# A two-stage Strassen kernel: third weight form from SyncE, products moved, token sums reordered

## Chip, cores and metric

The kernel runs on one core of a Trainium2 chip. The metric is the device time of one execution in microseconds; here the medians of several runs, and beside them one profiled execution with its own time.

## What is computed

An attention block without softmax (a retention with a decay per head) is followed by a feed-forward block with a product of two branches:

```python
# q, k, v: (8, 8, 576, 64) float32
scores = q @ k.T / sqrt(64)
ret = scores * where(i >= j, gamma[h] ** (i - j), 0)
x = (ret @ v)                      # brought to (8 * 576, 8 * 64) = (4608, 512)
a = x @ w1                         # w1, w2: (512, 1024)
b = x @ w2
out = ((a * b) @ w3) @ w_out       # w3: (1024, 1024), w_out: (1024, 512)
```

All of it is float32. The kernel forms w3 @ w_out once (tile w3o), so that a token passes two products: the "up" products x @ w1 and x @ w2, whose elementwise product is kept in tile ab, and the "down" product ab @ w3o.

## The kernel before

**Tiling.** The 8 batches are taken two at a time; a pair has 5 chunks of tokens (one of 64, four of 128), numbered g = 0 to 19 over the four pairs. For a chunk the attention part loads q, k and v, scales them, transposes q and k, and makes scores (`score`, L224, with the mask product L236 on DVE), the running state (`state`, L240) and the output x (`pv`, L278), which lands in tiles xT of 192 tokens of both batches. Twelve such blocks of tokens exist. The first four go through a plain Strassen product (`up`, L507); the other eight in four *groups* of two blocks, gr = 0 to 3, through two nested levels of Strassen (`up2`, L1008). All edits are in the part that handles groups, from about 350 us on.

**A group.** `token_forms` (L942) makes the sums of the two blocks of x that Strassen needs, all on POOL (`tt`, L948). First the differences inside xT, then six sums into tile T (which is a part of ra), then one difference b12 in place and two sums into tile E, then the sum E4 (the function `rest`, L964; for group 0 it is called later by hand, L1182, for the others inside), then a difference inside T, and six sums from T into tiles U. E and E4 serve the steps P1, P2, P7 and P3 of a half (below), T and U the steps P6, P4 and P5.

A group then has 14 *steps* (n = 0 to 13; two halves h of seven Strassen products in the order P1, P2, P6, P7, P4, P5, P3). A step (`up2`) has seven inner products on PE (L1028), each with two weight blocks, accumulated in PSUM tiles p1, p5 (pool acc, 5 banks) and p6 (pool seed, 2 banks). DVE adds the banks to tile c (one of four cc tiles in rotation, `plus`, L1035), ACT copies, and POOL adds earlier cc tiles into this one (`more`, L1031). The last inner product of a step and its adds (the inner function `rest`, L1082) are put behind and issued inside the next step by `finish` (L991). In the step P5, called the *joined* step here (`both` is not empty), the result goes into two cc tiles at once, so POOL has four sums instead of two and DVE two adds per bank (L1038).

**Products of results.** When a step completes a quarter of a and b, entries are added to the list `results` (L1090); `multiply(most)` (L995) takes up to that many of them and issues for each the DVE product L1003, ab <- cc * cc, whose two inputs are in SBUF. `up2` calls it near its end (L1076): at most 1 in a joined step, at most 2 in the others. A cc tile is free again after its second product.

**Weights.** The 14 weight forms (896 KB each) were stored in HBM (`kept`). A ring of three slots in SBUF holds the forms of this step and the next ones. `open_second` (L921) makes the ring and issues the first two forms on SP; after that every step issues one form on POOL (`next_forms`, L935, called at L1053). POOL's queue also holds the scaling of q (`scale_blocks`, L175, instruction L181) and loads of v and k (L93). SP's queue holds, right behind the first forms, the loads of q for the next chunks, 16 pieces per chunk (`load_blocks`, L160, L171). The program gives SP's transfers eight completion semaphores in turn.

**Output stage.** After the 14 steps come three `down` calls (L625). Each has seven products on PE (L637) over two tiles of 128 tokens, in the order 1 (A11), 7 (S3), 2 (A12), 6 (S2), 5 (S1), 4 (A22), 3 (S4). The sums S3, S2, S1 and S4 of ab are DVE instructions L607, L611, L613 and L679, with both inputs in SBUF. S2 and S1 need products of results from the last two steps.

**The order.** The order on each engine is written out by hand (`manual_schedule`): the loop from L1196 deals a number of steps to each chunk g (`dealt`, L1195: 3, 4, 4, 3, 3, 7, 7, 3, 7, 7), so a group's steps end at g = 13, 16 and 19, and the last group's after the loop. At the first three of these (`if g in ready`, L1225) the loop issues `pv`, then `finish` and `multiply` for everything that is left, then the state and the scores of the next chunk (there is none at g = 19), then it queues the next group. In the next round `token_forms` for the next group follows behind the first `down`. In the first `down` behind the last steps (L668 to L675) `finish` and `multiply` are called again, which matters for the last group alone. Queues run in order, and each engine stops at the first instruction whose input isn't there.

Of the kernel before, what the change touches and what calls it, by code (L numbers as in the profile page):

```python
# [19 lines left out]
def kernel(  # L20
# [875 lines left out]
    def weight_of(slot, nm, w):  # L896
        lo = {"A11": 0, "A12": P, "S3": 4 * P, "A22": 5 * P, "S1": 8 * P, "S4": 9 * P, "S2": 12 * P}[nm]
        lo += w * (P if nm == "S2" else 2 * P)
        return slot[:, lo:lo + P]

    order = ("P1", "P2", "P6", "P7", "P4", "P5", "P3")
    ring, sent, steps, free = [], [0], [0], []
    groups = [(m, m + 1) for m in range(4, len(every), 2)]

    def flush():
        while spread:
            spread.pop(0)()
# [13 lines left out]
    def open_second():  # L921
        nonlocal acc
        flush()
        acc_part.close()
        acc = ctx.enter_context(tc.tile_pool(name="acc", bufs=5, space=PSUM, reuse_waits="tile"))
        pools["seed"] = ctx.enter_context(tc.tile_pool(name="seed", bufs=2, space=PSUM, reuse_waits="tile"))
        ra = wp.tile([P, 32 * P], F32, tag="wA1", name="ra")
        cs = wp.tile([P, 2, 4, 2, TB], F32, tag="wS1", name="cc")
        ring.extend([ra[:, :FORM], ra[:, FORM:2 * FORM]])
        free.extend(cs[:, j] for j in range(2))  # L930
        live["first"] = [ra[:, 2 * FORM + j * DM // 2:2 * FORM + (j + 1) * DM // 2] for j in range(2)]
        for _ in range(2):
            next_forms(nc.sync)

    def next_forms(engine=nc.gpsimd):  # L935
        n = sent[0]
        if n < 14 * len(groups):
            nm = NAMES.index(OPERANDS[order[n % 7]][0])
            engine.dma_start(ring[n % 3], kept[n % 14 // 7][nm])  # L939
            sent[0] += 1  # L940

    def token_forms(gr):  # L942

        x = [live["xT", m] for m in groups[gr]]
        T, E, U = live["T2"], live["E"], live["U"]

        def tt(out, in0, in1, op=ALU.subtract):
            nc.gpsimd.tensor_tensor(out=out, in0=in0, in1=in1, op=op)  # L948

        for s in range(2):  # L950
            tt(x[s][:, :2, 1], x[s][:, 2:, 1], x[s][:, :2, 1])
        b11, b21 = (x[0].rearrange("p (r c) b t -> p r c b t", c=2)[:, :, c] for c in range(2))
        b12, b22 = (x[1].rearrange("p (r c) b t -> p r c b t", c=2)[:, :, c] for c in range(2))
        sums = [(T[:, s, 1], x[s][:, :2, 1], x[s][:, :2, 0], ALU.add) for s in range(2)]
        sums += [(T[:, s, 0], x[s][:, 2:, 1], T[:, s, 1]) for s in range(2)]
        sums += [(T[:, s, 2], x[s][:, 2:, 0], T[:, s, 1]) for s in range(2)]
        for args in sums:
            tt(*args)
        tt(b12, b22, b12)
        tt(E[:, 1], b12, b11, ALU.add)  # L960
        tt(E[:, 0], b22, E[:, 1])
        forms = {}

        def rest(b11=b11, b21=b21, b22=b22, b12=b12):  # L964
            if "E4" not in live:
                live["E4"] = pools["carry"].tile([P, KF, P], F32, tag="carry", name="e4").rearrange(
                    "p f n -> p (f n)")[:, :4 * TB].rearrange("p (r b t) -> p r b t", r=2, b=2)
            E4 = live["E4"]
            tt(E4, b21, E[:, 1])
            for nm, (r, b) in {"B11": (0, 0), "B21": (1, 0), "T3": (0, 1), "B22": (1, 1)}.items():  # L970
                forms[nm] = {"B11": b11[:, r, b], "B21": b21[:, r, b], "B22": b22[:, r, b], "T3": b12[:, r, b],
                             "T1": E[:, 0, r, b], "T2": E[:, 1, r, b], "-T4": E4[:, r, b]}

        if gr:
            rest()
        tt(T[:, 1, :, 0], T[:, 1, :, 1], T[:, 1, :, 0])
        for k in (slice(0, 2), 2):
            u = [U[j] if k != 2 else (U[3][:, 0], U[3][:, 1], U[4][:, 0])[j] for j in range(3)]
            b11, b21, b12, b22 = (T[:, s, k, c] for s in range(2) for c in range(2))
            tt(u[1], b12, b11, ALU.add)  # L980
            tt(u[0], b22, u[1])
            tt(u[2], b21, u[1])
            for i, nm in enumerate(("T1", "T2") if k != 2 else ("-T4",)):
                part = [y[:, i] if k != 2 else y for y in (b11, b21, b22, b12, *u)]
                forms[nm] = dict(zip(("B11", "B21", "B22", "T3", "T1", "T2", "-T4"), part))
        live["B2", gr] = forms
        return rest
# [20 lines left out]
    def up2(gr, n):  # L1008

        h, key = n // 7, order[n % 7]  # L1010
        slot = ring[steps[0] % 3]
        if not steps[0]:

            for _ in range(2):
                t = pools["seed"].tile([P, 2, TB], F32, tag="seed", name="seed")
                nc.tensor.matmul(t.rearrange("p a t -> p (a t)"), ident, live["w3o"][:, 0, :2 * TB],
                                 start=True, stop=True)
        B = live["B2", gr][OPERANDS[key][1]]
        steps[0] += 1
        c = free.pop(0)  # L1020
        sums2[key] = c
        add = {"P2": "P1", "P6": "P1", "P7": "P6", "P4": "P7", "P3": "P6"}.get(key)
        add = sums2[add] if add else None
        both = [sums2["P6"], sums2["P7"]] if key == "P5" else []

        def product(ps, a, b, new=False):
            for w in range(2):
                nc.tensor.matmul(ps[:, w, :], weight_of(slot, a, w), B[b], start=(new and w == 0), stop=True,  # L1028
                                 skip_group_check=True)

        def more(into, of, part):  # L1031
            o, i = into[:, part], of[:, part]
            nc.gpsimd.tensor_tensor(out=o, in0=o, in1=i, op=ALU.add)  # L1033

        def plus(ps, j, with_add=None):  # L1035
            if both:
                for o in both:
                    nc.vector.tensor_add(o[:, j], ps, o[:, j])  # L1038
            elif with_add is not None:
                nc.vector.tensor_add(c[:, j], ps, with_add[:, j])  # L1040
            else:
                nc.scalar.copy(c[:, j], ps)

        p1 = acc.tile([P, 2, TB], F32, tag="acc", name="up")
        product(p1, "A11", "B11", True)
        p6 = pools["seed"].tile([P, 2, TB], F32, tag="seed", name="seed")
        nc.scalar.copy(p6, p1)  # L1047
        store()
        p5 = acc.tile([P, 2, TB], F32, tag="acc", name="up")
        product(p5, "S1", "T1", True)  # L1050
        nc.scalar.copy(c[:, 3], p5)  # L1051
        finish()
        next_forms()  # L1053
        if loads:
            loads.pop(0)()
        product(p6, "S2", "T2")
        nc.scalar.copy(c[:, 1], p6)
        if beside:
            beside.pop(0)()
        for o in both:  # L1060
            more(o, c, 3)
        if add is not None:
            more(c, add, 3)
        product(p1, "A12", "B21")
        plus(p1, 0, add)
        product(p5, "S4", "B22")
        if add is not None:
            more(c, add, 1)
        for o in both:
            more(o, c, 1)  # L1070
        product(p6, "S3", "T3")
        plus(p6, 3, c)
        plus(p5, 1, c)
        if both:
            free.append(c)
        multiply(1 if both else 2)  # L1076
        if n == 13:
            results.append((gr, h, 0, 1, c, 1))
        if aside:
            aside.pop(0)()  # L1080

        def rest():  # L1082
            product(p6, "A22", "-T4")
            plus(p6, 2, add)
            if key in ("P6", "P3"):
                free.append(sums2["P1" if key == "P6" else "P6"])
            done = {"P2": (0, 0), "P4": (1, 0), "P5": (1, 1), "P3": (0, 1)}.get(key)
            if done:
                z = sums2["P7"] if key == "P5" else c
                results.extend((gr, h, *done, z, half) for half in ((0,) if n == 13 else (1, 0)))  # L1090

        behind.append(rest)

    real = (up, up2, down)

    def add_group(gr):
        X, Y = groups[gr]
        todo.extend((up2, gr, n) for n in range(14))
        todo.extend([(down, (X, 0), (X, 1)), (down, (X, 2), (Y, 2)), (down, (Y, 0), (Y, 1))])
# [96 lines left out]
    for g in range(2 * NC, G):  # L1196
# [27 lines left out]
        pv(g)()  # L1224
        if g in ready:  # L1225
            finish()
            multiply()
        if g + 2 < G:
            load(g + 2, "v", nc.gpsimd)
            if (g + 2) % NC != NC - 1:  # L1230
# [1 line left out]
        if g + 1 < G:  # L1232
            state(g + 1)
            score(g + 1)
        if g in ready:
            add_group(ready[g])
        if g == G - 1:
            token_forms(ready[g])
# [45 lines left out]
```

## Time and profile before

| | |
|---|---|
| median of 3 runs | 850.87 us (846.77 to 853.91) |
| the profiled execution's own time | 850.68 us |
| its span, first to last instruction | 848.9 us |
| mean granted TensorE clock | 0.989 |
| idle time of PE, by the span and its busy time | 29.6 us |
| idle time of PE before the product L1028 behind POOL sums into e | 3.7 us |
| products of results L1003 on DVE | 64, mean 796 ns |
| sums for token forms of 384 elements, xT and ra into ra (16) | mean 1237 ns |
| forms of weights issued by SP and by POOL | 2 and 54 |
| a form from issue to landing, median | 5.0 us |

The profile follows one execution instruction by instruction. A row of a timeline or a group names the source line, the engine, the operation, the tile written and the tiles read, the shape, and then the count, the duration and the idle time of the engine just before it with what ended that idle time. PE's list of waits adds these idle times up by pairs of lines. A wait for several semaphores is put down to the one that came last. The table of windows gives, for stretches of time, the busy time of an engine, the share of the full TensorE clock that was granted, and what the DMA engines moved.

### The profile page before, as it was taken

To read this page: it belongs to the slowest core of one execution; us is meant where nothing else is said; L and a number is where in the kernel's file an instruction comes from. 1 tells how busy PE (TensorE), PEld (TensorE's weight loads), DVE (VectorE), ACT (ScalarE), POOL (GpSimd) and SP (SyncE) were. 2 spreads that over 40 slices of the span, in tenths; PEclk is the share of its full clock that TensorE was granted. 3 is DMA by queue.
4 is the path that set the end of the run, shared out by engine and by line. 5 is a ranking of instruction groups with operands and counts; after the bars stand their busy time and mean duration, and the time that the engine had idled before them with its cause. 6 is when DMAs were issued, how large, how long until landed. Compare 5 with 4: busy or idle time off the path is not lost.

```text
span 848.9 us, 15774 instructions
## 1 busy us (share of the span) xinstructions
PE 819.3 (97%) x6085; PEld 738.1 (87%) x6085; DVE 541.2 (64%) x887; ACT 283.2 (33%) x581; POOL 325.6 (38%) x330
## 2 busy tenths in 40 slices
PE   7899999999999999979998999999999999999998
PEld 6889999644989998869998889998899998899987
DVE  4899999991644477615657644759735768446653
ACT  4777556670111101033343024342034331033300
POOL 1100010001104181395545935556916468445500
PEclk8999999999999999999999999999999999999999
DMA  9995454436046487979786147787275452245401
GB/s 193 217 224 128 77 150 125 126 98 112 1 98 125 75 220 251 307 209 220 190 229 167 44 93 228 201 238 177 58 156 183 140 208 69 77 148 189 159 25 51
DMA packets 201291, 126.96 MB, mean 150 GB/s; under 512 B 161272, under 2 KB 183032, under 8 KB 201216
## 3 DMA queue, kind: packets, MB, share of 16 engines
q1 hardware_dynamic: 170944, 50.14, 29.1%
q0 software_dynamic: 11776, 63.71, 23.0%
q10 hardware_dynamic: 18496, 12.10, 5.3%
q8 instruction: 48, 0.79, 0.4%
q14 instruction: 27, 0.22, 0.1%
HBM read 103.62 MB, written 22.28 MB: 148 GB/s over the span
## 4 chain that ended last, share of the span: by engine, by line
PE 79%; DMA 7%; DVE 7%; issue 3%; SPq 2%; ACT 1%; POOL 0%; ACTq 0%; DVEq 0%; POOLq 0%
PE po L637 24%; PE up L1028 15%; PE up L524 13%; PE seed L1028 11%; PE ps L477 6%; DMA ld_v<-in_v_dram 3%; PE xps L299 3%; PE sc L233 3%; DMA ra<-kept 2%; PE xps L274 1%; SPq L171 1%; DVE c L529 1%; DVE ab L1003 1%; DMA bl_q<-in_q_dram 1%; PE st L255 1%
## 5 line engine op out<-in xcount | busy, mean ns | idle before, releaser
L637 PE MATMUL po<-w3o,ab 128*128 128x256 f32 x552 | 125.0, 381 | 1.4 <-DVE ot L641 0.5
L637 PEld LDWEIGHTS po<-w3o,ab 128*128 128x128 f32 x552 | 103.9, 190 | 17.4 <-DVE ot L641 1.2
L1033 POOL TENSOR_TENSOR cc<-cc 128x384 f32<-128x384 f32 x112 | 109.3, 1001 | 4.1 <-ACT cc L1051 2.4
L1040 DVE TENSOR_TENSOR cc<-seed,cc 128x384 f32<-128x384 f32 x88 | 48.7, 553 | 72.9 <-PE seed L1028 68.5
L181 POOL TENSOR_TENSOR bl_q<-bl_q,gqs 128x512 f32<-128x512 f32 (+1 forms) x30 | 30.8, 1048 | 127.7 <-DMA bl_q<-in_q_dram 91.8
L939 POOL DMA_DIRECT2D ra<-kept x54 | 30.6, 567 | 124.1 <-PE seed L1028 103.3
L1028 PE MATMUL up<-xT,ra 128*128 128x192 f32 x384 | 74.2, 330 | 0.6 <-DMA ra<-kept 0.6
L1040 DVE TENSOR_TENSOR cc<-up,cc 128x384 f32<-128x384 f32 x88 | 48.4, 550 | 36.8 <-PE up L1028 31.5
L524 PE MATMUL up<-xT,wA 128*128 128x192 f32 x384 | 70.4, 327 | 0.0
L529 DVE TENSOR_TENSOR c<-up,c 128x384 f32<-128x384 f32 x80 | 44.0, 550 | 38.9 <-PE up L524 38.3
L1028 PEld LDWEIGHTS up<-xT,ra 128*128 128x128 f32 x384 | 64.4, 192 | 2.0 <-DMA ra<-kept 0.9
L236 DVE TENSOR_TENSOR pm<-sc,mask 128x512 f32<-128x512 f32 (+1 forms) x80 | 45.4, 626 | 32.1 <-PE sc L233 32.0
L637 PE MATMUL po<-wB,forms 128*128 128x256 f32 x288 | 65.2, 379 | 0.5 <-DVE forms L611 0.5
L524 PEld LDWEIGHTS up<-xT,wA 128*128 128x128 f32 x384 | 63.4, 190 | 1.1 <-issue 0.5
L637 PEld LDWEIGHTS po<-wB,forms 128*128 128x128 f32 x288 | 54.6, 190 | 8.2 <-PE po L637 0.8
L1047 ACT COPY seed<-up 128x384 f32<-128x384 f32 x56 | 25.9, 463 | 100.1 <-PE up L1028 46.6
L1028 PE MATMUL seed<-e,ra 128*128 128x192 f32 x256 | 52.9, 337 | 5.2 <-DVE cc L1040 2.9
L1028 PE MATMUL up<-ra 128*128 128x192 f32 x288 | 55.1, 328 | 1.9 <-DMA ra<-kept 1.9
L477 PE MATMUL ps<-wo,w3T 128*128 128x512 f32 x128 | 55.1, 592 | 0.0
L204 POOL TENSOR_TENSOR ld_v<-ld_v,gk 128x1024 f32<-128x1024 f32 (+1 forms) x9 | 17.1, 1899 | 90.5 <-DMA ld_v<-in_v_dram 90.5
L679 DVE TENSOR_TENSOR ab<-ab,forms 128x512 f32<-128x512 f32 x17 | 17.1, 1008 | 53.3 <-PE po L637 53.3
L1028 PEld LDWEIGHTS seed<-e,ra 128*128 128x128 f32 x256 | 43.7, 194 | 7.8 <-DVE cc L1040 3.6
(127 smaller groups left out, 1597.2 us busy)
## 6 DMA issues: line engine op xcount, KB each, us to landing
ra<-kept POOLq DMA_DIRECT2D x54, 896.0 KB, 5.0
raw<-in_moe_w_dram SPq DMA_DIRECT2D x72, 128.0 KB, 3.0
bl_q<-in_q_dram SPq DMA_DIRECT2D x216, 32.0 KB, 3.2
out_dram<-ot ACTq DMA_DIRECT2D x54, 128.0 KB, 2.3
bl_k<-in_k_dram SPq DMA_DIRECT2D x136, 32.0 KB, 2.4
raw<-in_moe_w_dram SPq DMA_DIRECT2D x16, 256.0 KB, 6.0
ld_k<-in_k_dram SPq DMA_DIRECT2D x8, 512.0 KB, 5.9
raw<-in_moe_w_out_dram SPq DMA_DIRECT2D x32, 128.0 KB, 2.7
```

What stands on the lines that cost most here:

```text
L181: nc.gpsimd.tensor_tensor(out=part, in0=part, in1=gqs[:, :, n0:n0 + n].unsqueeze(3).to_broadcast([P, NP, n, BL]), op=ALU.mult)
L233: nc.tensor.matmul(sc[j][:sz, p, :sz], kT[hs, b, p, :sz], qT[hs, b, p, :sz], start=True, stop=True)
L236: nc.vector.tensor_mul(pm[:sz, b, j, :, :sz], sc[j][:sz, :, :sz], mask[:sz, :sz].unsqueeze(1).to_broadcast([sz, NP, sz]))
L477: nc.tensor.matmul(ps, live["w3T", ft][:, g, :], live["wo"][:, g, :], start=(g == 0), stop=(g == KF - 1))
L524: nc.tensor.matmul(ps[:, w, :], a[:, w, r, :], b[:, r, :], start=(new and w == r == 0), stop=(w == r == 1), skip_group_check=True)
L529: nc.vector.tensor_add(c[:, to], ps, c[:, sb])
L637: nc.tensor.matmul(ps[nm], a[A][:, f, :], live["W"][B][:, f, :], start=(f == 0 and not on), stop=(f == NP - 1), skip_group_check=True)
L939: engine.dma_start(ring[n % 3], kept[n % 14 // 7][nm])
L1028: nc.tensor.matmul(ps[:, w, :], weight_of(slot, a, w), B[b], start=(new and w == 0), stop=True, skip_group_check=True)
L1033: nc.gpsimd.tensor_tensor(out=o, in0=o, in1=i, op=ALU.add)
L1040: nc.vector.tensor_add(c[:, j], ps, with_add[:, j])
L1047: nc.scalar.copy(p6, p1)
```

## The change

It has four parts. `open_second` issues three forms on SP instead of two, and `up2` issues a form only if fewer than two are ahead, so that the first step issues none and all later ones are as they were. In `token_forms` the six sums into T come behind b12, E and (but for group 0) E4, instead of ahead of them; since they then read the changed b12, the difference inside T (one POOL instruction of 576 elements) falls away. A joined step issues no product of results; the entry is taken by one of the next steps, so four instead of three are left at the end of a group. And at the end of a group the products that are left come behind the state and scores of the next chunk, so on DVE behind the four mask products L236.

```diff
@@ open_second
-        for _ in range(2):
+        for _ in range(3):
             next_forms(nc.sync)
@@ token_forms
         sums += [(T[:, s, 2], x[s][:, 2:, 0], T[:, s, 1]) for s in range(2)]
-        for args in sums:
-            tt(*args)
+
         tt(b12, b22, b12)
         tt(E[:, 1], b12, b11, ALU.add)
         tt(E[:, 0], b22, E[:, 1])
...
         if gr:
             rest()
-        tt(T[:, 1, :, 0], T[:, 1, :, 1], T[:, 1, :, 0])
+        for args in sums:
+            tt(*args)
         for k in (slice(0, 2), 2):
@@ up2
         finish()
-        next_forms()
+        if sent[0] < steps[0] + 2:
+            next_forms()
         if loads:
...
             free.append(c)
-        multiply(1 if both else 2)
+        if not both:
+            multiply(2)
         if n == 13:
@@ the loop over chunks
         if g in ready:
             finish()
-            multiply()
         if g + 2 < G:
             load(g + 2, "v", nc.gpsimd)
...
             state(g + 1)
             score(g + 1)
         if g in ready:
+            multiply()
             add_group(ready[g])
```

## The prediction

> **What bounds the kernel now.** I read part 1 of the page first, then the list of waits of PE, then the timelines of PE, POOL and DVE around each wait, and the table of windows for the granted clock.
>
> ```profile
> PE 819.3 (97%) x6085; PEld 738.1 (87%) x6085; DVE 541.2 (64%) x887; ACT 283.2 (33%) x581; POOL 325.6 (38%) x330
> ```
>
> PE is the bound. The change removes no matmul, so it acts on PE's idle time and on the clock alone. From 360 us on, where all edits lie, the waits that the edits can reach are these (line, what ended the wait, total us, times, longest):
>
> ```profile
> PE seed L1028 <- DVE cc L1040: 2.9, 3, 1.3
> PE up L1028 <- DMA ra<-kept: 2.5, 2, 1.9
> PE up L1028 <- POOL e L948: 2.2, 1, 2.2
> ...
> PE sc L233 <- DVE kT L190: 1.7, 1, 1.7
> PE seed L1028 <- POOL e L948: 1.5, 1, 1.5
> ...
> PE sc L233 <- DVE cc L1040: 0.7, 1, 0.7
> ...
> PE po L637 <- DVE forms L611: 0.5, 1, 0.5
> ```
>
> PE's timeline places them. At the start of group 0 PE waits 2.25 us until 369.74 (POOL e), 1.50 until 377.73 (POOL e, the last token form) and 1.91 until 383.16 (weight form 2). The DVE waits follow the joined step P5: in group 0's end 0.78 (462.73) and 1.72 (465.37), in group 1's middle 0.68 (546.22), in its end 0.79 (585.10), in group 3's middle 1.28 (776.93).
>
> Behind them stands a product of results (L1003) that usually takes 0.55 us and sometimes 2.7:
>
> ```profile
> L1003 DVE TENSOR_TENSOR ab<-cc x64: 529/549/2743, 390.7 to 811.9; 128x384 f32<-128x384 f32 x64
> ```
>
> Five of the eight in joined steps took 2.7 (456.96, 540.90, 579.32, 662.23, 772.28), while POOL added cc tiles. How DVE and POOL hinder each other is best seen at the end of group 2 (DVE, then POOL; the columns are start, duration, instruction):
>
> ```profile
> 706.34 3.58 DVE L1003 TENSOR_TENSOR ab<-cc 128x384 f32<-128x384 f32 x3
> 709.96 1.37 DVE L611 TENSOR_TENSOR forms<-ab 128x512 f32<-128x512 f32 x1
> ...
> 715.80 1.96 DVE L611 TENSOR_TENSOR forms<-ab 128x512 f32<-128x512 f32 x1
> ```
>
> ```profile
> 709.47 5.53 POOL L948 TENSOR_TENSOR ra<-xT,ra 128x384 f32<-128x384 f32 x4
> 715.08 2.13 POOL L948 TENSOR_TENSOR xT<-xT 128x768 f32<-128x768 f32 x1
> ```
>
> L611 takes 0.69 us beside an idle POOL, 1.37 beside POOL's 384-element sums, 1.96 beside a 768-element one: the two engines take turns, one whole instruction each. The masks (L236, one input from PSUM) take 0.68 beside the same POOL work: they do not take turns.
>
> [...] Here 2.25 us of idling sufficed. In the table of windows (PE busy, granted clock, DMA share, GB/s) the clock falls behind the first wait:
>
> ```profile
> 366.00:368.00 2.00, 1.49 (x7) 1.00 0.95 389
> 368.00:370.00 2.00, 0.26 (x1) 1.00 1.10 224
> 370.00:372.00 2.00, 2.00 (x8) 0.50 0.35 58
> ```
>
> It falls so too in 384 to 386 and 466 to 468; the 1.28 us at 776.9 cost no clock. [...] the windows 366 to 368 and 380 to 382 show 389 and 386 GB/s while forms move, for either issuer.
>
> **Part by part.** The sum is made against the profiled execution (span 848.9, its own time 850.68; the median of the three runs is 850.87, so nothing is to be shifted).
>
> *Start of group 0 (third form, token order).* POOL's sums of xT into ra take 1.95+3.86 = 5.8 us; put behind E they let E end at 369.68-5.8 = 363.9, before PE comes at 367.5. That wait goes, but PE then stands at -T4's form (E4), which ends only 1.4 us earlier (377.68 to 376.3, the 576-element sum of 1.40 that is gone). So the first two waits give 1.4, and PE sits 4.4 us in one piece. Form 2 leaves SP at about 363.6 instead of POOL at 377.62; at 896 KB and 389 GB/s it is in by 372, and PE wants it at about 379.7: the 1.91 go. Together 3.3. What is late next: SP's 16 pieces of bl_q for chunk 11, 363.55 to 374.62, now queue behind 0.9 MB more, 2.4 us; they land near 380, and POOL's in-order queue holds behind them: scaling 2.08 (to 382.1), a form's issue 0.6, the first cc sum 0.98 (383.7), then DVE's add 0.56 (384.2), which frees the seed bank for PE's last product of the second step. Before it began at 385.44, and half clock cost it another 0.8. Gain 385.4+0.8-384.2 = **2.0**; between 0.3 (pieces 2 us later still) and 4 (not late, clock kept). SP's extra issue is 0.34, POOL's saved one 0.6. The test in L1053 drops one issue in the first step only. The shorter token sums of groups 1 to 3 (1.4 to 1.9 us of POOL each) are worth nothing: the forms are ready at 495.2 and wanted at 510.3, and similarly later; without that cover they would give that much.
>
> *Joined steps.* One product fewer in each of 8. In the middles (n=5) two PE waits go: 0.68+1.28 = **2.0**. The others had no wait behind them. The product reappears in steps 6 to 8, in DVE gaps of 0.77: nothing.
>
> *Ends of groups (n=12, 13, then the output stage).* Now four products are left instead of three, and they come after the masks. Group 2 is the clearest: it has no score, so the products start at 706.4 as before; but POOL, after its xT difference (to 706.97), now has 768-element sums: 1.80 each plus 0.32 for DVE's turn. Products end at 707.3, 709.4, 711.5, 713.7; L611 at 713.7+1.80+0.44 = 716.0. PE's product of S2 needs L611: 711.48 before, 716.0 after, **+4.5**. L613 (717.4) is then hidden by that product. A 5 us wait halves the clock for about 3.4 us, +1.7; half of it counted: **+5.4**.
> Group 1: PE arrives 0.79 sooner; masks 587.2 to 589.65; then turns with POOL's scaling (to 589.85), two xT differences and 768-element sums: products end 590.2, 591.5, 592.7, 594.9, L611 597.2, L613 599.5. S2 at 597.25 (594.86 before), S1 at 599.5 (596.59): **+2.9**, with half clock +4.1; taken **+3.5**.
> Group 0: without the 2.7 stall the score starts at 462.8 instead of 465.37, masks end 466.3. But bl_q of chunk 15 is loaded when qT's transpose frees its buffer, 2.6 sooner as well, so POOL's scaling starts at 465.8, not 468.44, and the same turns follow: L611 472.4, L613 474.65; S1 474.7 against 475.95. -1.2, or +0.5 with half clock: **-0.4**.
> Group 3: POOL is idle; the fourth product ends at 812.95, L611 at 813.7, S2 is due at 814.29: **0**.
>
> Sum: -2.0-2.0-0.4+3.5+5.4 = +4.5: 850.68+4.5 = **855**. That is inside 1%, about what a measurement of this kernel can tell from no change.
>
> **Rivals.**
> 1. *The turns don't bite* (the products slip in ahead of POOL's long sums, as the one at 699.98 did in 0.55 us beside cc sums). Then group 0 gains 4.2 (S1 471.8), group 1 1.5, group 2 0.5, the start up to 3.7, the middles 2.0: -11.9, **839**. For it: that row. Against: 709.96 and 715.80.
> 2. *Slower: DVE is passed over.* In the five rows of 2.7 us DVE waited through two POOL sums, not one. If that happens to each of the four products and L611 at the ends, L611 comes at about 721.7 in group 2 (+10.2), +9.2 in group 1, +6 in group 0; with half clock +3 and -4 from the rest: +24, **875**. It decides once DVE loses more than about one extra 768-element sum per end. Against: in 706 to 720 no row lost two.
> 3. *Only one more turn.* POOL's long sums begin late enough, or overlap the masks, so that an end costs one 384-element turn (+0.6, +1.2) and group 0 gains 1.2: with the start and the middles -3.4, **847**.
> That the change does not do what it says is excluded: the order of instructions shows the third issue on SP, four products behind four masks, and L948 in the new order.
>
> **How the numbers follow.** Main case 0.62 (own range 849 to 863), rival 3 0.18, rival 2 0.12, rival 1 0.08. Slower by over 1% (above 859.4): rival 2 and a sixth of the main case, 0.22. Faster by over 1% (below 842.3): 0.08. The rest 0.70. Range 845 to 864, which leaves out rivals 1 and 2.
>
> **What would show it.** Right: no PE wait on POOL e before 370, one of about 4.4 us near 372 to 376; no wait on form 2; L1003 never at 2.7 in a joined step; DVE's four L1003 and L611 at the ends of groups 1 and 2 stretched to 1.5 to 2.1 us each, followed by "PE po L637 <- DVE forms L611" waits of 3 to 5 us, with half clock behind. Wrong: those waits under 1 us (rival 1 or 3), or L611 later than 720 in group 2 (rival 2); or bl_q of chunk 11 so late that PE stands at step 2 as long as it did for the form.

## The result, and the profile after

| | before | after |
|---|---|---|
| median of 12 runs each, us | 851.18 (846.77 to 862.94) | 856.07 (854.31 to 857.89) |
| ratio, 95% interval | | 1.0057 (1.0033 to 1.0081) |
| span and own time of the profiled execution | 848.9, 850.68 | 856.2, 857.89 |

The change costs half a per cent: 5.4 us over the profiled execution that the sum was made on, where 4.5 were forecast, and 4.9 between the two medians. The twelve times of before spread over 16.2 us, those of after over 3.6. Ratios here and below are estimated without runs more than 1.5% above the fastest of their kernel, so they differ a little from those of the medians. The first line of the page of after, and the head of PE's list of waits from 355 us on (line, what ended the wait, total us, times, longest):

```profile
PE 824.5 (96%) x6085; PEld 741.3 (87%) x6085; DVE 534.4 (62%) x887; ACT 282.5 (33%) x581; POOL 317.2 (37%) x325
```

```profile
PE po L637 <- DVE forms L611: 9.9, 2, 5.0
PE seed L1028 <- POOL e L948: 2.6, 1, 2.6
PE seed L1028 <- DVE cc L1040: 2.1, 1, 2.1
```

PE is busy 5.2 us longer over the same 6085 matmuls, which is lower clock (0.982 granted, 0.989 in before; about half of it lies ahead of all edits), and 9.9 us of waiting, where before had 0.5, stand in two places: L637 behind L611, the product of S2 at the ends of groups 1 and 2. The waits on DVE behind the joined steps and on form 2 are gone. Where the time went is read by lining up the same PE matmul in both traces; the "shift" is how much later it starts in after.

| place | forecast, us | change of the shift, us |
|---|---|---|
| before any edit (to 356) | | +3.2 |
| start of group 0 (to 390) | -2.0 | -2.7 |
| end of group 0 | -0.4 | -4.4 |
| middles of groups 1 and 3 | -2.0 | -1.4 -1.5 |
| a form's landing in group 1 (558) | 0 | +0.7 |
| end of group 1 | +3.5 | -0.9 +4.5 +3.1 |
| middle of group 2 | 0 | -0.6 |
| end of group 2 | +5.4 | +4.5 +2.7 |
| sum from 356 us on, before rounding | +4.5 | +4.2 |

The 3.2 us ahead of any edit are variation between two executions. Where a row has several numbers for one end, they are, in order, the scores that come sooner (group 1 alone), the wait for S2, and half clock. DVE, then POOL, at the end of group 2 (start, duration, instruction):

```profile
708.06 7.27 DVE L1003 TENSOR_TENSOR ab<-cc 128x384 f32<-128x384 f32 x4
715.37 2.17 DVE L611 TENSOR_TENSOR forms<-ab 128x512 f32<-128x512 f32 x1
```

```profile
710.84 2.00 POOL L948 TENSOR_TENSOR e<-xT 128x768 f32<-128x768 f32 x1
712.92 4.07 POOL L948 TENSOR_TENSOR e<-xT,e 128x768 f32<-128x768 f32 x2
```

Four products take 7.27 us: 1.03 for the first, 2.15 for each of the others, because each waits through one of POOL's 768-element sums (2.00 us each while it does). L611 ends at 717.54, and PE, which came at 712.7, waits 4.96 us. The table of windows (PE busy, granted clock, DMA share, GB/s) shows the price of such a wait at the end of group 1:

```profile
590.00:592.00 2.00, 0.00 (x0) 1.00 0.44 104
592.00:594.00 2.00, 0.00 (x0) 0.84 0.00 0
594.00:596.00 2.00, 1.97 (x5) 0.50 0.00 0
```

The clock stays at half for 6.83 us, from 593.37 to 600.20. At the end of group 0 the same four products meet hardly any of POOL's work:

```profile
464.24 2.48 DVE L236 TENSOR_TENSOR pm<-sc,mask 128x512 f32<-128x512 f32 x4 [0.28 <-PE sc L233]
466.64 2.38 DVE L1003 TENSOR_TENSOR ab<-cc 128x384 f32<-128x384 f32 x4
469.06 0.99 DVE L611 TENSOR_TENSOR forms<-ab 128x512 f32<-128x512 f32 x1
```

```profile
467.76 1.74 POOL L181 TENSOR_TENSOR bl_q<-bl_q,gqs 128x256 f32<-128x256 f32 x2 [4.32 <-DMA bl_k<-in_k_dram]
```

POOL's scaling comes at 467.76, when two products are done, and its long sums come later still. In before it came at 468.44:

```profile
468.44 1.20 POOL L181 TENSOR_TENSOR bl_q<-bl_q,gqs 128x256 f32<-128x256 f32 x2 [5.32 <-DMA bl_k<-in_k_dram]
```

### The profile page after: what moved, and what is told of

Read it like the earlier page. It is cut to its first block, busy times and chain, and to the rows that moved or that the text cites. A ratio compares the mean times of both kernels' runs of the same rounds, so it can differ in the third digit from the quotient of the medians.

```text
span 856.2 us, 15776 instructions
## 1 busy us (share of the span) xinstructions
PE 824.5 (96%) x6085; PEld 741.3 (87%) x6085; DVE 534.4 (62%) x887; ACT 282.5 (33%) x581; POOL 317.2 (37%) x325
## 4 chain that ended last, share of the span: by engine, by line
PE 81%; DMA 6%; DVE 6%; issue 2%; SPq 2%; ACT 1%; POOL 1%; ACTq 0%; DVEq 0%; POOLq 0%
PE po L637 24%; PE up L1028 15%; PE up L524 12%; PE seed L1028 12%; PE ps L477 6%; PE xps L299 4%; PE sc L233 3%; DMA ld_v<-in_v_dram 2%; PE xps L274 2%; DVE ab L1003 2%; DVE c L529 1%; PE st L255 1%; SPq L171 1%; DMA out_dram<-ot 1%; DMA ra<-kept 1%
## 5 line engine op out<-in xcount | busy, mean ns | idle before, releaser
L637 PE MATMUL po<-w3o,ab 128*128 128x256 f32 x552 | 125.0, 381 | 1.9 <-DVE ab L607 1.0
L637 PEld LDWEIGHTS po<-w3o,ab 128*128 128x128 f32 x552 | 103.9, 190 | 17.9 <-DVE ot L641 1.4
L1040 DVE TENSOR_TENSOR cc<-seed,cc 128x384 f32<-128x384 f32 x88 | 48.7, 553 | 71.5 <-PE seed L1028 61.7
L637 PE MATMUL po<-wB,forms 128*128 128x256 f32 x288 | 71.0, 403 | 9.9 <-DVE forms L611 9.9
L637 PEld LDWEIGHTS po<-wB,forms 128*128 128x128 f32 x288 | 58.5, 204 | 19.7 <-issue 10.6
L1040 DVE TENSOR_TENSOR cc<-up,cc 128x384 f32<-128x384 f32 x88 | 48.5, 551 | 39.0 <-PE up L1028 30.9
L236 DVE TENSOR_TENSOR pm<-sc,mask 128x512 f32<-128x512 f32 (+1 forms) x80 | 45.6, 629 | 37.2 <-PE sc L233 37.2
L1047 ACT COPY seed<-up 128x384 f32<-128x384 f32 x56 | 26.0, 464 | 95.7 <-PE up L1028 42.8
L641 DVE TENSOR_TENSOR ot<-po,ot 128x256 f32<-128x256 f32 x72 | 30.4, 422 | 33.6 <-PE po L637 32.9
L477 PEld LDWEIGHTS ps<-wo,w3T 128*128 128x128 f32 x128 | 24.3, 190 | 30.1 <-issue 29.7
```

The costliest lines, as they stand in the source:

```text
L236: nc.vector.tensor_mul(pm[:sz, b, j, :, :sz], sc[j][:sz, :, :sz], mask[:sz, :sz].unsqueeze(1).to_broadcast([sz, NP, sz]))
L477: nc.tensor.matmul(ps, live["w3T", ft][:, g, :], live["wo"][:, g, :], start=(g == 0), stop=(g == KF - 1))
L637: nc.tensor.matmul(ps[nm], a[A][:, f, :], live["W"][B][:, f, :], start=(f == 0 and not on), stop=(f == NP - 1), skip_group_check=True)
L641: nc.vector.tensor_add(ot[:, to[0], to[1]], ps[nm], ot[:, sb[0], sb[1]])
```

## Experiments

The theory: the ends of groups 1 and 2 cost what they do because DVE's products take turns with POOL's long sums. Rivals: that a fourth product, or its place, costs this whatever POOL does; and, later, that other parts of the change carry its gains. Each kernel is compared with runs of before on the same chip, whose median there was 851.1 to 856.6 us. After was not run again beside them; where a kernel is set against after, it is by their traces.

**a1_old_order: shorter turns at the ends.**

```diff
+        for args in sums if gr else []: tt(*args)
         tt(b12, b22, b12)
...
-        for args in sums:
-            tt(*args)
+        for args in [] if gr else sums: tt(*args)
+        if gr: tt(T[:, 1, :, 0], T[:, 1, :, 1], T[:, 1, :, 0])
```

> The changed kernel with the old token order in groups 1 to 3 (six sums of 384 elements into T first, the 576-element difference back); group 0 keeps the new order. Theory 'length of POOL's turns': at the ends of groups 1 and 2 each DVE product waits through 1.43 us instead of 2.0 us, so L611 ends near 591.6 and 714.9 instead of 593.9 and 717.5, the two waits for S2 fall from 4.9 and 5.0 to about 2.4 and 2.2 us, and 5 us come back, up to 10 if the clock stays full: 846 to 851, likeliest 848 (ratio to before 0.996). Rival 'a fourth product in DVE's queue is what costs, whatever POOL does': the waits stay near 4.9 and the time near 856.

Measured 846.83 us, ratio 0.9934 (0.9910 to 0.9958). DVE at the end of group 2, and the windows of group 1:

```profile
704.22 4.84 DVE L1003 TENSOR_TENSOR ab<-cc 128x384 f32<-128x384 f32 x4
709.09 1.37 DVE L611 TENSOR_TENSOR forms<-ab 128x512 f32<-128x512 f32 x1
```

```profile
590.00:592.00 2.00, 0.00 (x0) 1.00 0.54 122
592.00:594.00 2.00, 1.96 (x9) 1.00 0.06 11
```

Four products take 4.84 us instead of 7.27. The two waits for S2 add to 4.4 us (2.64 and 1.72) instead of 9.9, and the clock stays full behind both. The cost went with the length of POOL's turn: a product took at most 1.35 us here, and 2.16 in after.

**a2_gate: POOL's sums begin when S1 is made.**

```diff
     def token_forms(gr):
+        if gr > 1: nc.gpsimd.tensor_copy(out=live["E"][:, 0, 0, 0, :1], in_=pair_of((groups[gr - 1][0], 0), (groups[gr - 1][0], 1))[0]["S1"][:, 0, :1])
...
-        if g == G - 1:
-            token_forms(ready[g])
     g = G
+    work(1)
+    token_forms(3)
```

The copy of one element into E reads S1, so POOL waits for DVE there. The rest of the edit puts the sums of group 3 behind the `down` call that makes the S1 in question.

> The changed kernel with one tiny POOL copy ahead of the token sums of groups 2 and 3 that reads S1, so that POOL starts these sums only when DVE has made S1; no other instruction moves. Theory 'turns between DVE and POOL': the four products run in 0.55 us each behind the masks (ends of groups 1 and 2), L611 and L613 in 0.69; no wait for S2 there, no half clock: 4.9 + 3.1 + 5.0 + 2.7 = 15.7 us come back, 840 (ratio 0.987). The token sums end some 8 us later, which 23 us of idle POOL cover. Rival 'the queue is what costs': DVE's four products, L611 and L613 alone still end after PE needs S2, waits of 2 us or more stay and the time is 850 or more.

Measured 841.40 us (839.65 to 841.55), ratio 0.9877 (0.9821 to 0.9932). DVE and POOL at the end of group 2:

```profile
699.58 1.95 DVE L1003 TENSOR_TENSOR ab<-cc 128x384 f32<-128x384 f32 x4
701.57 0.69 DVE L611 TENSOR_TENSOR forms<-ab 128x512 f32<-128x512 f32 x1
```

```profile
703.05 0.18 POOL L943 COPY e<-forms 128x1 f32<-128x1 f32 x1 [7.52 <-DVE forms L613]
```

Alone, four products take 1.95 us and L611 0.69. Both waits and both stretches of half clock are gone: against after, PE gains 5.1 + 3.1 us at group 1 and 5.1 + 2.7 at group 2, 16.0 in all where 15.7 were expected. The rival falls: a fourth product behind the masks is free when POOL holds still.

**a3_ahead: products ahead of the scores again.**

```diff
             finish()
+            multiply()
...
-            multiply()
             add_group(ready[g])
```

> The changed kernel with the products that are left issued ahead of the next chunk's state and scores again. Theory 'turns': the end of group 1 loses its wait, since the four products then run before POOL's long sums begin (4.9 + 3.1 = 7 to 8 us back, of which the later masks may cost PE up to 1); the end of group 2 has no scores, nothing changes there (5.0 wait, half clock 2.7); group 0 loses up to 1.5. 848 to 851, likeliest 849. Rival 'order plays no part, a fourth product does': the wait for S2 at group 1 stays above 4, and the time at 856.

Measured 849.34 us, ratio 0.9962 (0.9936 to 0.9988). Group 1 gets its 8.2 us back (5.1 wait, 3.1 clock); at group 2, which has no scores, the wait of 5.0 us stays. The place behind the scores costs only through whom the products meet there.

**a4_joined: the product back in the joined steps.** A miss.

```diff
-        if not both:
-            multiply(2)
+        multiply(1 if both else 2)
```

> The changed kernel with the product back in the joined steps, so three are left at a group's end. Theory 'turns': one turn of 2.15 us fewer at the ends of groups 1 and 2 (waits for S2 about 2.8 instead of 4.9 and 5.0), the 1.4 us of waits in the middles of groups 1 and 3 come back, and at the ends of groups 0 and 1 the scores wait behind a 2.7 us product again (+1 to +2.5 in group 0, +0.8 in group 1): 854 to 857, likeliest 856. Rival 'the joined step's product is what the change gains by': 860 or more.

Measured 865.12 us, ratio 1.0165 (1.0114 to 1.0217): 9 us above the forecast, and the rival's number. DVE and POOL in the last joined step of group 2:

```profile
706.65 3.69 DVE L1003 TENSOR_TENSOR ab<-cc 128x384 f32<-128x384 f32 x1
```

```profile
706.42 0.57 POOL L939 DMA_DIRECT2D ra<-kept  x1 [0.28 <-PE seed L1028]
707.01 1.95 POOL L1033 TENSOR_TENSOR cc<-cc 128x384 f32<-128x384 f32 x2
708.92 0.99 POOL L948 TENSOR_TENSOR xT<-xT 128x384 f32<-128x384 f32 x1
```

The product began at 706.65, during POOL's issue of a form and ahead of three sums, and ran behind all three. It is not taking turns here; it is passed over. In group 0 such a product (2.71 us at 456.68) holds up the transpose of k, so the scores come 2 us later, so the masks end at 468.7 and not 466.7, and then three products, L611, L613 and L679 all fall among POOL's long sums and take 2.17, 2.18 and 2.29 us, where they took 0.99, 1.37 and 1.48 in after: 6.2 us at that end, where 1 to 2.5 were expected. At group 1 the product fewer saved 2.7 us. At group 2 it saved nothing: that end became 2.2 us longer, with L607 late (a wait of 1.86).

**b3_no_joined: that part alone, on the kernel before.**

```diff
-        multiply(1 if both else 2)
+        multiply(0 if both else 2)
```

> The kernel before with one part of the change alone: no product of results in a joined step. Theory 'the 2.7 us product there holds up all that DVE has behind it': the middles gain 2.0 us, the scores at the end of group 0 come 1.7 to 2.5 us sooner, those of group 1 0.8; four products at the ends of groups 1 and 2 cost one more turn of 1.4 us each, in group 2 a wait for S2 of about 1.7: 3 to 6 us less than before (ratio 0.993 to 0.997). Rival 'the product only moves to where it costs the same': ratio 1.000 within the interval.

Measured 845.76 us, ratio 0.9910 (0.9877 to 0.9943): more than expected. From 402 us on its trace gains 6.8 us over before's: 4.5 at the end of group 0, 1.2 and 1.5 in the middles, 0.9 at the scores of group 1, less 1.3 at group 2. So one part of the four is worth 7 to 8 us by itself (7.7 by the ratio, whose interval allows 5 to 10), and the rest of the change spends it.

**d1_issue_on_ACT: why is the joined product passed over?**

```diff
-        next_forms()
+        next_forms(nc.scalar if both else nc.gpsimd)
```

> The kernel before with the weight form of each joined step (8 of 54) issued by ACT instead of POOL; nothing else moves. It asks why the product in a joined step takes 2.7 us, through two POOL sums, where products elsewhere wait for one. Theory 'POOL's issue of a form just ahead of the two sums makes DVE lose its turn': all eight L1003 in joined steps at 1.6 us or less, and the time 1 to 4 us below before. Rival 'two sums issued back to back pass DVE over in any case': five of eight stay at 2.7, time within 2 us of before.

Measured 845.13 us, ratio 0.9893 (0.9858 to 0.9927); no L1003 is longer than 1.37 us. DVE and POOL in the joined step at 467:

```profile
466.84 0.55 DVE L1003 TENSOR_TENSOR ab<-cc 128x384 f32<-128x384 f32 x1
```

```profile
463.42 2.90 POOL L1033 TENSOR_TENSOR cc<-cc 128x384 f32<-128x384 f32 x3
467.24 0.59 POOL L939 DMA_DIRECT2D ra<-kept  x1 [0.91 <-PE seed L1028]
```

All eight durations are the theory's; the gain, some 9 us, is well above the 1 to 4 expected. But they don't prove it: freed of waiting for the form's slot, POOL had made its sums by 466.33 and was idle when the product came. What is shown is that the product is cheap when it does not meet them (0.55 us).

**Two clusters of times.** The runs of b3_no_joined fall into 11 from 841.5 to 846.3 us and 9 from 851.0 to 856.2; those of d1_issue_on_ACT into two tens, up to 843.2 and from 847.0. The profiles of both are from the upper cluster. DVE and POOL of b3_no_joined:

```profile
359.76 6.74 DVE L679 TENSOR_TENSOR ab<-ab,forms 128x512 f32<-128x512 f32 x1 [4.62 <-PE po L637]
```

```profile
360.19 1.94 POOL L948 TENSOR_TENSOR ra<-xT 128x384 f32<-128x384 f32 x2
362.10 3.85 POOL L948 TENSOR_TENSOR ra<-xT,ra 128x384 f32<-128x384 f32 x4
366.02 2.14 POOL L948 TENSOR_TENSOR xT<-xT 128x768 f32<-128x768 f32 x1
```

L679 began while a difference inside xT ran, was then passed over by six sums and ran at 365.95, in the first pause POOL made (some 80 ns, ahead of a sum that overwrites what the sixth had read). The start of group 0 was 8.4 us longer for it, half clock included. The profile of d1_issue_on_ACT shows the same: 6.59 us at 359.54, behind the same six sums. In the profile of before:

```profile
355.81 1.62 DVE L679 TENSOR_TENSOR ab<-ab,forms 128x512 f32<-128x512 f32 x1 [3.49 <-PE po L637]
```

When L679 comes goes with what happens to it. In before, f4_gaps and b1_form it began 0.08 us ahead of, 0.33 us into and 1.15 us ahead of POOL's first difference inside xT, and took 1.62, 1.21 and 2.69 us, no more than one whole sum behind the one that ran. In b3_no_joined and d1_issue_on_ACT it began 1.5 and 1.6 us behind that start, while the second difference ran. No kernel moved it on purpose. The next three kernels take the clusters apart.

**f4_gaps: pauses among the six sums.**

```diff
-        for args in sums:
+        for args in sums if gr else [sums[k] for k in (0, 2, 4, 1, 3, 5)]:
```

> The kernel before with the six sums into ra of group 0 in another order, so that two of them stand right behind the sum that they read (a pause of about 80 ns between two dependent sums in these traces, none between independent ones). Theory 'DVE gets its turn only at a pause once it is passed over': L679 at 2.6 us or less in every run, the upper cluster at most 3 us above the lower one, ratio 0.994 to 0.997. Rival 'pauses play no part': L679 of 4 us or more and two clusters 8 us or more apart, as in before.

Measured 850.86 us (848.05 to 854.71), ratio 0.9983 (0.9959 to 1.0008); before spread in the same comparison from 846.07 to 861.11. The upper cluster is gone, and the range is 6.7 us wide instead of 15; the median gains less than expected. L679 took 1.21 in the profile, but there it came early (above), so this profile does not test the pause; the times do, and g1_kept_parts below.

**f1_order_gr0: the new token order in group 0 alone.** A miss in time.

```diff
-        for args in sums:
-            tt(*args)
+        for args in sums if gr else []: tt(*args)
...
-        tt(T[:, 1, :, 0], T[:, 1, :, 1], T[:, 1, :, 0])
+        for args in [] if gr else sums: tt(*args)
+        if gr: tt(T[:, 1, :, 0], T[:, 1, :, 1], T[:, 1, :, 0])
```

> The kernel before with the new token order in group 0 only. In two profiles (of b3_no_joined and d1_issue_on_ACT) DVE's L679 at 359.5 us took 6.6 to 6.7 us, through six POOL sums into ra in a row, and the start of group 0 was 8 to 9 us longer than in the profile of before, where it took 1.6; the times of these kernels fall into two clusters some 9 us apart. Theory 'the six independent sums pass DVE over in about half of the executions': with E's sums there instead, L679 stays at 1.6 us or less in every run, and the times make one cluster, 847 to 851 (ratio to the mixed runs of before about 0.993). Rival 'the two clusters come from elsewhere': times spread over 12 us or more as before's do, ratio above 0.997.

Measured 855.88 us (850.03 to 859.20), ratio 1.0051 (1.0029 to 1.0074). One cluster, and L679 at 1.06 in the profile, but 5 us above the forecast. Its trace has two places: PE waits 3.4 us for E4, 2.4 for form 2 and 3.2 behind L1040, so the start is 2.0 us longer than in the profile of before; and the joined product at 700 us was passed over (3.68 us, where before's took 0.55), 3.9 us at the end of group 2. That the start is longer for want of the third form on SP is not shown: b2_token_order has the same code there, and its start is 3.1 us shorter than before's.

**b1_form: the third form on SP alone.** Its edits are those of `open_second` and of L1053 in the change.

> The kernel before with the third weight form on SP alone. Theory 'this part is worth little by itself': the wait for form 2 goes (1.9 us), and bl_q for chunk 11 lands 2 us or more later, which costs the same at DVE's L1040; ratio 0.997 to 1.001, and the times keep their two clusters, since POOL's six sums stand where they stood. Rival 'the third form alone makes the start better': ratio 0.995 or less, or one cluster.

Measured 858.09 us, ratio 1.0062 (1.0028 to 1.0096). The two clusters stay (ten runs up to 856.2, ten from 860.0), as expected; the ratio is above the expected range. Its trace, from the lower cluster, stands 3.0 us behind before's; the joined product at 699 us again (3.69) costs it 3.9 at the end of group 2.

**b2_token_order: the new order in all groups alone.** Its edits are those of `token_forms` in the change.

> The kernel before with the new token order alone (all groups). Theory 'turns with long sums': at the start 1.4 us are gained; at the ends of groups 1 and 2 the products and L611 wait through 2.0 us sums, a wait for S2 of 2 to 4 us in group 2 and 1 to 3 in group 1, with half clock behind one or both: 2 to 7 us more than before (ratio 1.002 to 1.008). Rival 'the order of the sums is free at the ends': 1 to 2 us less (ratio 0.998).

Measured 859.90 us, ratio 1.0062 (1.0035 to 1.0088), within the theory's range. The wait for S2 in group 2 is 3.9 us, with 1.7 of half clock; its joined product was passed over too (3.69 us at 699.7), so not all of it is the order's. Group 1 kept its time, where the theory had a wait of 1 to 3 us.

**c1_start: two moves at the start of group 0, on a2_gate.**

```diff
-        if gr:
-            rest()
-        for args in sums:
+        def late():
+          rest()
+          for args in sums:
...
-        return rest
+        return late if not gr else late()
...
-            scale_blocks(g + 1)
+            aside.append(lambda: scale_blocks(g + 1)) if g == 2 * NC else scale_blocks(g + 1)
```

> The kernel with the gate (a2_gate), and two moves at the start of group 0: E4 ahead of the six sums into T and of the sums into U, and POOL's scaling of q for chunk 11 behind the sums of cc tiles of the second step instead of ahead of them. Theory 'at the start PE stands for E4's place in POOL's queue, and then for bl_q through POOL's queue': the waits of 2.6 and 2.5 us and most of the half clock behind them go, 5 to 8 us below a2_gate: 834 to 837 (ratio 0.98 to before). Rival 'another input is as late': T, U or the third form stops PE there instead, and the time is within 2 us of a2_gate's 841.

Measured 840.88 us (838.60 to 848.84), ratio 0.9854 (0.9789 to 0.9919): the rival's number. By 390 us PE was 8.9 us ahead of a2_gate, and by 404 it had given 7.0 of them back. ACT there:

```profile
397.10 1.28 ACT L202 ACTIVATE ld_v<-ld_v,gk 128x128 f32<-128x128 f32 x4 [3.90 <-DMA ld_v<-in_v_dram]
398.29 0.47 ACT L1047 COPY seed<-up 128x384 f32<-128x384 f32 x1
```

ACT's scaling of v waits for a load that lands at 397.1, the copy L1047 stands behind it in ACT's queue, and PE waits 2.53 us for the copy. A load bounds the start next; it was only hidden by the other waits.

**g1_kept_parts: what pays, without the rest.** On the kernel before: the edit of b3_no_joined, that of f4_gaps and that of a2_gate.

> The kernel before with no product in a joined step, the order of f4_gaps for the six sums of group 0, and the gate of a2_gate ahead of the token sums of groups 2 and 3; neither the third form on SP nor the new token order nor products behind scores. Theory 'what pays is that DVE's products meet an idle POOL; the other parts of the change are not needed': b3_no_joined's lower cluster (841.5 to 846.3) less the 1.7 us of its wait for S2 in group 2, in one cluster: 839 to 843, within 2 us of a2_gate (ratio 0.985 to 0.990). Rival 'the third form and the new order carry part of a2_gate's gain': 845 or more.

Measured 841.45 us (840.07 to 841.87), ratio 0.9853 (0.9778 to 0.9928): as fast as a2_gate and faster than before beside it (853.14), its four runs within 1.8 us. DVE and POOL at the start of group 0:

```profile
358.30 2.14 DVE L679 TENSOR_TENSOR ab<-ab,forms 128x512 f32<-128x512 f32 x1 [4.83 <-PE po L637]
```

```profile
358.90 0.98 POOL L948 TENSOR_TENSOR ra<-xT 128x384 f32<-128x384 f32 x1
359.97 2.30 POOL L948 TENSOR_TENSOR ra<-xT,ra 128x384 f32<-128x384 f32 x2
```

L679 came much where it had come in b3_no_joined, 1.3 us behind the start of the first difference inside xT. It waited for the sum that was running, was passed over by the next (358.90), and got in at the pause between 359.88 and 359.97: the two sums behind take 2.30 us, 0.35 more than in f4_gaps.

## Why the prediction was right, term by term

The result was right, and so was the mechanism: turns with 768-element sums at the ends of groups 1 and 2, waits at L637 on L611, half clock behind. a1_old_order, a2_gate and a3_ahead show it from three sides. The terms of the sum were mis-sized, and the errors nearly cancel: three gained more than forecast, two cost more. That 855 came within about 1 us of the median is luck.

- *End of group 0, -0.4 forecast, -4.4 measured.* The step that failed was "POOL's scaling starts at 465.8, not 468.44, and the same turns follow". SP's loads of q did begin 2.3 us sooner (458.60 against 460.90), and seven of the eight pieces had landed by 464.85, where before's last landed at 468.28. But the eighth was issued at 463.16, after POOL had issued a load of v (256 KB) at 462.58, and landed at 467.55, 0.45 us behind that load, and POOL's scaling came only 0.7 us sooner than in before, not 2.6. By the landing of the others it could have begun near 465, as the prediction had it (an estimate); one piece decided this end. So what the missing 2.7 us product gave was kept whole: 1.0 at the step's last product, 1.8 at the scores, 1.6 at the output stage. b3_no_joined gains 4.5 there with that part alone.
- *End of group 1, +3.5 forecast, +6.7 measured.* POOL's scaling came at 582.8, while the masks ran (587.9 in before), so it didn't take turns with the products; POOL reached its 768-element sums by the third product and L613 met one as well. And half clock cost 3.1 us, where half of 1.2 was counted: it lasted 6.83 us and not about 3.4. That was an estimate: in before each stretch of half clock from 360 us on lasts 3.41 us, but behind waits of 2.25, 1.91 and 1.72 us.
- *End of group 2, +5.4 forecast, +7.2 measured.* The wait was right to the tenth (+4.5). Half clock cost 2.7, where half of 1.7 was counted. It lasted 6.83 us here too, and it should have been counted in full: a2_gate got both stretches back.
- *Start of group 0, -2.0 forecast, -2.7 measured.* The path was right in its parts: no wait on E, none on form 2, a wait of 2.05 us on L1040 in its place. The wait on E4 was 2.57 and not 4.4, since PE came 3.5 us later than reckoned and E4 only 1.6. In the traces of a1_old_order, a2_gate and a3_ahead the same code gains 1.7, 0.7 and 1.1 us here against before; the term is no sharper than that.
- *Middles, -2.0 forecast, -2.9 measured.* The two waits are gone, as reasoned; what gave the rest is not shown.

Of the rivals, "the turns don't bite" fell with the two waits. "DVE is passed over" did not come about where it was placed: no product at an end lost two turns. But it was priced as a fate of after, while it is a fate of before: the products in joined steps and, to go by its near kernels, L679. The prediction read these 2.7 us rows and went no further than the PE waits right behind them. What was missed with them is the size of the gain from taking the product out of the joined steps, 9.0 us by a4_joined and 7.7 by b3_no_joined, and that the profile the sum was made on shows the good case twice (L679 1.62, the product at 699.98 0.55), where traces of its near kernels show 6.7 and 3.7. For L679 the clusters make it likely that this changes from one execution to the next; for the product no two executions of one kernel were profiled, so that is not shown.

What stays open is what decides between the two manners: one turn each, as at every end, or passed over, as in joined steps and in L679. The kernels f4_gaps and g1_kept_parts speak for a pause in POOL's work as the way out once passed over; no run shows what leads in. For joined steps the rows of before and a4_joined narrow it down: eight products there began 0.23 to 0.26 us into POOL's issue of a form, with a sum 0.33 to 0.36 us behind them. Seven ran behind all of the two or three sums that followed at once (2.71 to 2.74 us, and 3.69), and one, at 699.98 in before, ran at once (0.55) with three sums behind it. So the moment alone does not decide either.

## What to carry to other kernels

What a DVE instruction with two SBUF inputs cost here went with what POOL was doing: a product of 384 elements took 0.55 us beside an idle POOL, 1.35 beside sums of 384 elements (a1_old_order), 2.15 beside sums of 768 (after), and up to 3.69 where it was passed over (a4_joined); L679, of 512 elements, took 0.69 beside an idle POOL (345.19 in before) and 6.74 where it was passed over (b3_no_joined). So look for the stretch where PE waits on DVE, and keep POOL's long independent sums out of it, even with a one-element copy that makes POOL wait: here its sums ended some 4 us later, behind which POOL was still idle for 10 and 15 us in a2_gate's trace, and 16 us were gained at the two ends. And count half clock in full where a trace shows it behind such waits: behind those of 4.90 and 4.96 us in after, 5.0 in a3_ahead and 5.4 in b3_no_joined, 6.8 us of it followed each. Last, take from a spread of run times that one profile is not the kernel.

## What was not expected of the hardware

Which of the two engines waits did not go with which was there first: in b3_no_joined L679 began at 359.76, ahead of six POOL sums from 360.19 on, and ran behind the last of them (6.74 us); in a4_joined a product began at 706.65, 0.36 us ahead of three sums, and ran behind them (3.69 us).

The clock did not follow the length of a wait either (the clock by the table of windows):

| trace | wait of PE, us | clock behind it |
|---|---|---|
| before | 2.25 from 367.49 | half, 3.41 us from 370.01 |
| before | 1.91 from 381.25 | half, 3.41 us from 383.66 |
| before | 1.72 from 463.64 (and 0.78 until 462.73) | half, 3.41 us from 465.58 |
| after | 2.57 from 375.36 | half, 3.41 us from 378.33 |
| after | 2.05 from 384.43 | full (1.00 from 384 to 392) |
| a1_old_order | 2.64 from 589.41 | full (1.00 from 588 to 602) |
| after | 4.90 from 589.13 | half, 6.83 us from 593.37 |
| after | 4.96 from 712.73 | half, 6.83 us from 716.25 |

So a wait of 1.91 us in before was followed by half clock, and one of 2.64 us in a1_old_order was not. In before and after, from 360 us to the last matmuls, PE was idle for 1.91 to 3.41 of the 3.41 us ahead of each stretch of half clock. What sets the waits of 2.05 and 2.64 us apart from those is not shown.
